# A GLA and MLP-mixer kernel on one core: a second hand order of all instructions and loads

## The chip, the cores and the metric

The kernel runs on one core of a Trainium2 chip. The metric is device time in microseconds (us); lower is better. Every execution is one launch of the whole program.

## The reference

Two stages follow each other, for 4 batches, 8 heads, 768 steps and head size 48:

```python
# gated linear attention, per batch and head
for t in range(768):
    state = alpha[t][:, None] * state + outer(k[t], v[t])      # 48 x 48
    y[t] = q[t] @ state
x = y.transpose(0, 2, 1, 3).reshape(4, 768, 384)
# mixer
h  = maximum(x.transpose(0, 2, 1) @ w_tok1, 0) @ w_tok2        # tokens 768 -> 256 -> 768
u  = x + h.transpose(0, 2, 1)
h2 = maximum(u @ w_ch1, 0) @ w_ch2                             # channels 384 -> 1536 -> 384
out = u + h2
```

Inputs, weights and the output are float32.

## The kernel before

The attention is cut into 12 blocks `n` of 256 steps: three for each batch, so blocks 0 to 2 belong to batch 0 and blocks 9 to 11 to batch 3. A block has two halves (0 and 1) of 128 steps. Each operation has a name that ends in its block. In order of their dependence:

- `ld_at`, `ld_kt`, `ld_qt`, `ld_vt`: loads of alpha, k, q and v (384 KB each, issued by SP). `ldw_` loads a weight, `cw_` casts it to bf16 (L745 on ACT, L746 on DVE and POOL).
- `P`, `ln1`, `lnP`, `r1` (`ln` in blocks 0 to 2): products and logarithms of alpha. `cum` (`cumw`): cumulative sums by matmul. `E`, `IE`: their exponentials, on ACT.
- `k0a`, `q0r`: one factor into k and q (L692, L696). `kk`, `qq`: the scaled k and q (L700). `vb`, `vs`, `ka`, `kb`, `kc`: casts and copies between partitions.
- Blocks 0 to 5: `trk`, `trq`: transposes by PE (L712), and `evk`, `evq` bring them out of PSUM. Blocks 6 to 11: `dk`, `dq`: transposes by DMA (L725), and `pq` rearranges q's.
- `G0_`, `G1_`: the products of k and q of a half; `mask0_`, `mask1_` (DVE, L770) mask them. `K`: the sum of k times v; `s0_`, `sa`, `sm`: the new state. `i`, `y`: the output by matmul, `x` brings it out of PSUM.

The mixer of batch `b` has token matmuls `t1` and `t2` (L878, L883) with `ht` and `u` (L887) behind them; transposes of u (`up` and `ut` for batch 0, `ux` by DMA, L729, for the others); channel matmuls `c1_b_mc_half` (L902) into one PSUM bank each, `rt` behind them (L873 on ACT, L875 on DVE), `c2_b_i_q` (L907) in quarters, `o` (L911) and the store `st` (L624). The last tile of batch 3 is cut into two halves, `h0` and `h1`. In `c1` the halves of w_ch1 (`wc10` to `wc12` and `wc13` to `wc15`) serve the channel groups 0 to 5 and 6 to 11.

Nothing is scheduled when the program runs. A string `ORDER` lists every operation in the order in which it is emitted; the last letter is its queue: t PE, s ACT, v DVE, g POOL, y SP. Each queue runs its instructions in this order, and waits where an input or a buffer isn't there yet. `f3_trk0` is a filler: matmuls on zeros, as long as three of 512 columns, into a bank that nobody reads. A second list, `BUFS`, gives the buffer number of each value when it first appears (19 buffers for loads, 20 for `rt`, 8 banks of PSUM). So a load on SP waits until the last reader of its buffer is done, and all loads, transposes and stores behind it on SP wait with it. `GATES` is empty.

Copies and products on DVE and POOL that share a port take turns: each one waits for the last of the other engine that stands ahead of it in `ORDER`. This is made in `shared`:

```python
e, last = self.port_turn, self.port_last
if e:
    if last and last[0] != e:
        self.tc.add_manual_dep(i.ins, last[1].ins.name, ..., reason="shared port")
    self.port_last = (e, i)
```

It holds for P, k0a, q0r, kk, qq, vb, vs, ka, kb, kc, pq, sm and the weight casts, where they are on DVE or POOL.

Of the kernel before, what the change touches and what calls it, by code (L numbers as in the profile page):

```python
# [965 lines left out]
```

## Time and profile before

| what | value |
|---|---|
| time, median of 3 runs | 166.03 us (163.29 to 166.45) |
| time of the profiled execution | 164.76 us |
| its span, first to last instruction | 163.0 us |
| PE busy | 155.2 us, 95% of the span |
| DVE busy | 118.0 us, 72% |
| ACT busy | 95.7 us, 59% |
| POOL busy | 74.3 us, 46% |
| share of the chain that ended last: L907, L902 | 14% and 8%, both PE |
| read from HBM, written | 25.17 MB, 4.72 MB |

The span is counted from the first to the last instruction; the time of the execution is a little longer. Rows of a profile give a line of the kernel, an engine, an operation, and the tiles as out<-in. Matmuls are pipelined: the record of one of 384 columns is about 0.33 us long, while the next one starts sooner, so the busy time of PE is that of overlapping records. A value in square brackets is the time that the engine stood idle ahead of a row, with what ended it. Where an instruction waits for several things, the one named came last by the profile.

### The profile page before, as it was taken

The page shows a single profiled execution, that of the slowest core. Times are in us where ns is not written, and L with a number is a line of the kernel's source. Part 1 is how long each engine was busy: PE and PEld are TensorE (multiplying, and loading weights), DVE is VectorE, ACT ScalarE, POOL GpSimd, SP SyncE. Part 2 cuts the span into 40 slices and gives each one's busy share as a digit, 9 for nine tenths or more (in the row PEclk, how much of TensorE's full clock was granted, in tenths as well). Part 3 has the DMA queues.
Part 4 walks back from the last instruction along what each step waited for, and adds up shares of the span by engine and source line. Part 5 has one row for each costly group of instructions (what it writes and reads, how often), then busy time and mean ns, then how long its engine had stood idle before and what let it go on. Part 6 is the DMA issues. An engine that isn't in the chain of part 4 may idle for free. (4 is left out here: it accounts for less than half of the span.)

```text
span 163.0 us, 3969 instructions
## 1 busy us (share of the span) xinstructions
PE 155.2 (95%) x1560; PEld 97.2 (60%) x1560; DVE 118.0 (72%) x214; ACT 95.7 (59%) x178; POOL 74.3 (46%) x87
## 2 busy tenths in 40 slices
PE   7999989799999999999999999999799999999992
PEld 2456555556677676666666656666566655666661
DVE  6299993989989877587969855895698657162622
ACT  3888999789999964487777441495813201721000
POOL 5015593729294867469454278886830100000000
DMA  5999899989999999999999899989730136101133
GB/s 128 325 325 322 225 365 380 314 286 313 300 342 368 264 286 246 238 238 264 149 253 302 217 333 215 227 213 170 160 129 20 36 78 171 57 0 52 53 117 121
DMA packets 76130, 35.05 MB, mean 215 GB/s; under 512 B 70352, under 2 KB 74320, under 8 KB 76112
## 3 DMA queue, kind: packets, MB, share of 16 engines
q1 hardware_dynamic: 74960, 33.33, 77.9%
q10 hardware_dynamic: 1152, 1.48, 2.6%
q8 instruction: 12, 0.20, 0.5%
q14 instruction: 6, 0.05, 0.1%
HBM read 25.17 MB, written 4.72 MB: 183 GB/s over the span
## 5 line engine op out<-in xcount | busy, mean ns | idle before, releaser
L907 PE MATMUL ps<-wc,rt 128*128 128x384 bf16 (+1 forms) x300 | 52.4, 320 | 0.2 <-ACT rt L873 0.2
L902 PE MATMUL ps<-ut,wc 128*128 128x384 bf16 x288 | 50.3, 326 | 0.3 <-POOL wc L746 0.3
L907 PEld LDWEIGHTS <-rt 128*128 128x128 bf16 x300 | 28.0, 98 | 16.5 <-ACT rt L873 0.3
L902 PEld LDWEIGHTS <-wc 128*128 128x128 bf16 x288 | 27.1, 98 | 17.5 <-POOL wc L746 0.5
L873 ACT ACTIVATE rt<-ps 128x384 bf16<-128x384 f32 x54 | 24.9, 491 | 20.2 <-PE ps L902 19.6
L875 DVE TENSOR_SCALAR rt<-ps 128x384 bf16<-128x384 f32 x42 | 21.9, 553 | 12.7 <-PE ps L902 12.7
L770 DVE TENSOR_TENSOR gtm<-ps,mk 128x1024 bf16<-128x1024 f32 x24 | 28.4, 1217 | 1.7 <-PE ps L643 1.6
L911 DVE TENSOR_TENSOR o<-ps,u 128x384 f32<-128x384 f32 (+1 forms) x25 | 13.1, 535 | 5.9 <-PE ps L907 5.8
L887 DVE TENSOR_TENSOR u<-ps,x 128x384 bf16<-128x384 f32 x24 | 11.9, 550 | 6.4 <-PE ps L883 5.6
L700 POOL TENSOR_TENSOR pkk<-in,IE 128x768 bf16<-128x768 f32 x7 | 12.7, 1815 | 2.8 <-DVE in L692 2.5
L745 ACT CAST vb<-in 64x384 bf16<-64x384 f32 (+1 forms) x18 | 11.8, 654 | 2.5 <-DMA in<-in_v_dram 2.2
L643 PE MATMUL ps<-rt 128*64 128x384 f32 (+1 forms) x26 | 11.4, 537 | 1.1 <-DVE rt L541 1.1
L844 POOL TENSOR_TENSOR ss<-tmp,E 128x384 bf16<-128x384 f32 x9 | 7.5, 833 | 9.3 <-DVE tmp L841 9.1
L745 ACT CAST x<-ps 128x384 bf16<-128x384 f32 x15 | 7.0, 477 | 7.5 <-PE ps L643 7.5
L746 POOL CAST vb<-in 64x384 bf16<-64x384 f32 (+1 forms) x14 | 8.3, 594 | 5.8 <-PE ps L643 2.4
L878 PE MATMUL ps<-x,wt 128*128 128x384 bf16 x48 | 10.6, 325 | 0.3 <-ACT wt L745 0.3
L700 POOL TENSOR_TENSOR pkq<-in,E 128x768 bf16<-128x768 f32 x5 | 9.1, 1815 | 2.9 <-ACT IE L679 1.9
L692 POOL TENSOR_TENSOR in<-in,in 128x384 f32<-128x384 f32 x7 | 6.9, 998 | 6.3 <-DVE kt L746 3.2
L643 PE MATMUL ps<-tpq,tpk 48*64 48x128 bf16 (+1 forms) x288 | 8.5, 219 | 1.3 <-POOL tpq L746 0.8
L841 DVE TENSOR_TENSOR tmp<-ps,ss 128x384 f32<-128x384 f32 x16 | 8.8, 552 | 1.0 <-PE ps L643 0.4
L628 POOL TENSOR_TENSOR in<-in 128x384 f32<-128x384 f32 x8 | 7.9, 997 | 3.4 <-DVE ss L844 1.7
L883 PE MATMUL ps<-ht,wt 128*128 128x384 bf16 x48 | 9.3, 326 | 0.1
(95 smaller groups left out, 211.9 us busy)
## 6 DMA issues: line engine op xcount, KB each, us to landing
in<-in_alpha_dram SPq DMA_DIRECT2D x12, 384.0 KB, 5.8
in<-in_k_dram SPq DMA_DIRECT2D x12, 384.0 KB, 5.7
in<-in_q_dram SPq DMA_DIRECT2D x12, 384.0 KB, 5.1
in<-in_v_dram SPq DMA_DIRECT2D x12, 384.0 KB, 5.9
...
```

The lines of the kernel that those rows point to most:

```text
L643: return self.pe.matmul(out, lhsT=lhsT, rhs=rhs, start=start, stop=stop, skip_group_check=True)
L700: self.shared(self.eng[e].tensor_tensor(self.t(dst)[:, :, h0:h1, 0:D], self.t(src)[:, h0:h1].rearrange("p h s d -> p s h d"), bass.AP(tens ...
L745: return self.act.copy(d, s)
L770: self.nc.vector.tensor_tensor(self.t(gtm)[:, hf, :, :], self.pair(gp).rearrange("p a (j t) -> p (a j) t", t=128), bass.AP(tensor=m.tensor ...
L873: self.act.activation(d, s, AF.Relu)
L875: self.nc.vector.tensor_scalar_max(d, s, 0.0)
L878: self.pe.matmul(self.bank(bank)[:, 0:HD], lhsT=self.wt1[:, kc, m * 128 : m * 128 + 128], rhs=self.t(x), start=(kc == 0), stop=(kc == NS - 1))
L883: self.pe.matmul(self.bank(bank)[:, 0:HD], lhsT=self.wt2[:, kc, i * 128 : i * 128 + 128], rhs=self.t(hts[kc]), start=(kc == 0), stop=(kc = ...
L887: self.nc.vector.tensor_tensor(self.t(u)[:, i % 3], self.bank(bank)[:, 0:HD], self.t(x), ALU.add)
L902: self.pe.matmul(self.bank(bank)[:, 0:HD], lhsT=self.wc1[:, kc, mc * 128 : mc * 128 + 128], rhs=self.t(ut)[:, 3 * half : 3 * half + 3, kc, ...
L907: self.pe.matmul(self.bank(bank)[:, 0 : cz - ca], lhsT=self.t(rts[mc][0])[:, i * 128 : i * 128 + 128], rhs=self.wc2[:, mc, ca:cz], start=( ...
L911: self.nc.vector.tensor_tensor(self.t(o)[:, ca:cz], self.bank(bank)[:, 0 : cz - ca], self.t(u)[:, i % 3, ca:cz], ALU.add)
```

## The change

Only `ORDER` and `BUFS` are different; the operations, their sizes and their dependences are the same, apart from the fillers. The order of every queue is another from the first microsecond to the last, many operations change their engine, and buffers are numbered anew. On ACT there are now 196 operations (185 before), on DVE 189 (191), on POOL 69 (75), on SP 96 (99); eleven stores go out on ACT's queue instead of eight. Named by the change itself is the load of block 11's values: `ld_vt11` now stands on SP behind `dq10`. Three stretches of it: the start, the weights and first mixer, and blocks 9 to 11.

```diff
 ORDER = """
-ld_at0y ln0s ld_at1y f8_cumw0t f1_cumw0t cumw0t ln1s ld_kt0y IE0s cumw1t kk0v kb0v ld_qt0y E0s qq0v ld_vt0y IE1s vb0s
-ka0g f3_trk0t trk0t evk0v vs0_0v f3_trq0t trq0t kc0v vs1_0v E1s ld_kt1y kk1v f4_K0t K0t s0_0v sa1_0v evq0s f2_G0_0t
-G0_0t G1_0t ib0t mask1_0v ld_at2y ka1s ln2s ld_vt1y vb1s kb1g trk1t cumw2t IE2s kc1s sm1_0g ld_qt1y qq1v f3_trq1t
-trq1t vs0_1g E2s mask0_0v vs1_1s y1_0t f4_K1t K1t evq1v sa0_1v y0_0t ld_kt2y kk2g trk2t evk1s ld_qt2y qq2v G1_1t
-f1_trq2t trq2t x1_0s evk2s sm0_1v sa1_1v ld_vt2y G0_1t vb2g mask1_1v kc2g mask0_1v sm1_1g evq2s vs0_2s f4_K2t f1_K2t
-K2t x0_0s G0_2t G1_2t ld_at3y P3g ldw_wt11y cw_wt11s ib1t y1_1t vs1_2g sa0_2v mask0_2v ldw_wt10y cw_wt10s ia1t y0_1t
-t1_0_0_0t t1_0_0_1t x1_1s ia2t x0_1s y0_2t sm0_2g ib2t t1_0_1_0t t1_0_1_1t ld_at4y ln14s t1_0_1_2t x0_2s mask1_2v
-t1_0_1_3t y1_2t ldw_wt21y t1_0_0_2t x1_2v t1_0_0_3t t1_0_0_4t t1_0_1_4t t1_0_1_5t cw_wt21s P4g lnP4s ldw_wt20y
-cw_wt20g ht_0_1v t1_0_0_5t ld_kt3y k0a3v lnP3s cum3t ldw_wc15y ht_0_0s ldw_wc13y ldw_wc14y t2_0_2t t2_0_3t ld_vt3y
-t2_0_5t t2_0_1t u_0_2v t2_0_0t IE3s cum4t ln13s r13s u_0_3v up_0_1t E3s kk3g cw_wc15g t2_0_4t u_0_5v trk3t IE4s u_0_1v
-u_0_0v up_0_0t u_0_4v up_0_2t ut_0_0v ut_0_1s ut_0_2v cw_wc13g cw_wc14s c1_0_11_0t rt_0_11_0v vb3g vs0_3v E4s
-c1_0_8_1t ld_qt3y ka3s q0r3v ldw_wc11y kb3v evk3s ldw_wc10y c1_0_9_1t kc3s c1_0_10_1t qq3v rt_0_10_1v c1_0_8_0t
-ldw_wc12y cw_wc11g rt_0_8_1s vs1_3s rt_0_9_1s c1_0_11_1t cw_wc10g rt_0_8_0v rt_0_11_1v c1_0_10_0t rt_0_10_0s trq3t K3t
-ld_at5y ld_kt4y c1_0_9_0t evq3s c1_0_7_0t cw_wc12g ld_qt4y ld_vt4y s0_3v r14s ld_kt5y sa1_3v sm1_3g G0_3t rt_0_9_0s
-G1_3t mask0_3v mask1_3v rt_0_7_0s c1_0_1_1t c1_0_5_0t c1_0_0_1t ln15s c1_0_2_0t P5g c1_0_5_1t rt_0_5_0s rt_0_2_0v r15s
-rt_0_1_1s rt_0_5_1v rt_0_0_1s lnP5s c1_0_7_1t rt_0_7_1s c1_0_6_1t rt_0_6_1s c1_0_4_0t c1_0_3_1t k0a4g kk4v cum5t ib3t
-y1_3t c1_0_1_0t q0r4v qq4v c1_0_3_0t vb4s IE5s ka4v k0a5g E5s rt_0_3_1v trq4t rt_0_3_0v x1_3s trk4t evk4v rt_0_1_0s
-c1_0_2_1t rt_0_2_1v evq4s ldw_wc20y kb4s cw_wc20g c1_0_4_1t rt_0_4_0v G0_4t ld_qt5y q0r5g mask0_4v ldw_wc21y ld_vt5y
...
-u_2_5v u_2_4v ld_qt10y ux_2_1y lnP10s o_1_3v lnP11s c2_1_5_0t st_1_3y c2_1_5_1t c2_1_0_0t u_2_0v ln111s cum11t
-c2_1_0_1t c2_1_0_2t dq9y t2_2_1t u_2_1v cum10t c2_1_0_3t E11s k0a10g IE10s u_2_2v q0r10g E10s c2_1_5_2t c2_1_5_3t
-o_1_4v IE11s o_1_5v c1_2_10_1t kb9g rt_2_10_1v c1_2_7_1t rt_2_7_1v kk10g o_1_0v pq9v c1_2_1_1t c1_2_3_1t c1_2_8_1t
-vs0_9s qq10g ux_2_0y rt_2_8_1s c1_2_11_1t c1_2_0_0t dk9y c1_2_11_0t rt_2_3_1s G1_9t rt_2_11_1v G0_9t ka9s rt_2_1_1v
-ld_qt11y rt_2_0_0s r111s rt_2_11_0v vs1_9s mask1_9v c1_2_10_0t c1_2_9_0t c1_2_3_0t c1_2_6_0t rt_2_10_0s mask0_9v
-rt_2_6_0v kk11g kc9s K9t s0_9v rt_2_3_0s rt_2_9_0s c1_2_5_0t c1_2_1_0t c1_2_7_0t st_1_4y q0r11g c1_2_9_1t ib9t
-rt_2_5_0s rt_2_7_0v ld_vt11y vb11s rt_2_1_0v y1_9t rt_2_9_1s dq10y c1_2_8_0t rt_2_8_0s c1_2_5_1t rt_2_5_1s sa1_9v
-c1_2_4_0t rt_2_4_0s c1_2_2_0t qq11g c1_2_2_1t rt_2_2_1v pq10g dk10y G1_10t vb10s G0_10t mask1_10v sm1_9g mask0_10v
-y0_9t c1_2_0_1t vs0_10g dk11y rt_2_2_0s c2_2_0_0t c2_2_0_1t c2_2_0_2t c2_2_0_3t x1_9v rt_2_0_1v o_2_0v dq11y kb10s
-pq11g vs0_11v st_2_0y vs1_10s x0_9s G0_11t G1_11t mask0_11v c2_2_2_0t c2_2_1_0t c2_2_2_1t c2_2_2_2t ka10g ia10t y0_10t
-kc10s mask1_11v st_1_0s x0_10s K10t vs1_11g c2_2_2_3t sa0_10v sm0_10v sa1_10v c2_2_1_1t t1_3_0_0t t1_3_0_1t c1_2_6_1t
-kc11s c2_2_1_2t c2_2_1_3t sm1_10v st_1_5y K11t sa0_11v ib10t y1_10t rt_2_6_1s t1_3_0_2t t1_3_1_0t t1_3_1_1t ia11t
...
+ld_at0y ln0s ld_at1y ln1s ld_kt0y f8_cumw0t f1_cumw0t cumw0t IE0s E0s kk0v cumw1t IE1s ld_qt0y ld_vt0y f3_trk0t trk0t
+qq0v f1_trq0t trq0t ka0s kc0v E1s vb0v vs0_0s kb0v vs1_0v f3_K0t K0t ld_kt1y kk1v ka1g s0_0v evk0v evq0s f6_G1_0t
+G1_0t ld_at2y ld_vt1y trk1t ln2s cumw2t sa1_0v vb1s kb1g sm1_0g evk1s IE2s mask1_0v ib0t y1_0t kc1v ld_qt1y qq1v G0_0t
+x1_0v f1_trq1t trq1t vs0_1s mask0_0v vs1_1s E2s ld_kt2y kk2g K1t f1_y0_0t y0_0t sa0_1v sm0_1v evq1s trk2t kc2s sa1_1v
+f3_G1_1t G1_1t G0_1t ib1t ld_qt2y qq2g sm1_1g x0_0s ldw_wt10y cw_wt10s mask1_1v f2_trq2t trq2t ld_vt2y vb2s vs0_2g
+f3_K2t K2t evq2s ldw_wt11y y1_1t x1_1s ldw_wt20y evk2v cw_wt11g cw_wt20g mask0_1v sa0_2v sm0_2g G0_2t G1_2t ia1t y0_1t
+vs1_2s ia2t t1_0_0_0t t1_0_1_0t t1_0_1_1t mask0_2v t1_0_0_1t y0_2t x0_1s t1_0_0_2t t1_0_1_2t t1_0_1_3t ib2t ld_at3y
+t1_0_0_3t P3g ln13s x0_2s mask1_2v y1_2t ldw_wt21y cw_wt21g x1_2s t1_0_0_4t t1_0_1_4t f1_t1_0_1_5t t1_0_1_5t t1_0_0_5t
+ht_0_1v lnP3s ht_0_0s cum3t IE3s t2_0_2t u_0_2v r13s ld_at4y ln14s P4g lnP4s t2_0_1t u_0_1v ld_kt3y k0a3g ldw_wc13y
+t2_0_0t t2_0_3t t2_0_4t u_0_0v cum4t u_0_4v u_0_3v E3s t2_0_5t u_0_5v kk3g up_0_0t ut_0_0v cw_wc13s up_0_1t ut_0_1v
+up_0_2t trk3t ldw_wc15y IE4s ldw_wc14y cw_wc15g ut_0_2v cw_wc14s c1_0_10_0t ldw_wc11y ka3s c1_0_11_0t evk3v kc3v
+ld_vt3y cw_wc11s rt_0_10_0v ld_qt3y c1_0_8_1t vb3s E4s r14s rt_0_8_1v kb3g vs1_3g c1_0_7_1t rt_0_7_1v vs0_3v
+c1_0_11_1t rt_0_11_1s c1_0_6_1t rt_0_11_0s q0r3v qq3v rt_0_6_1v ldw_wc12y c1_0_9_0t rt_0_9_0s c1_0_8_0t cw_wc12g
+rt_0_8_0s c1_0_9_1t ldw_wc10y rt_0_9_1v ld_at5y P5g K3t cw_wc10s trq3t s0_3v c1_0_10_1t sa1_3v sm1_3g evq3s ld_kt4y
+c1_0_1_1t rt_0_1_1v c1_0_2_0t rt_0_10_1s rt_0_2_0s G1_3t G0_3t ln15s c1_0_2_1t mask1_3v lnP5s rt_0_2_1s c1_0_3_1t
+k0a4g rt_0_3_1s mask0_3v c1_0_4_1t ld_vt4y rt_0_4_1v vb4s c1_0_1_0t ld_qt4y kk4v rt_0_1_0s c1_0_6_0t r15s c1_0_0_1t
+rt_0_0_1s c1_0_7_0t ldw_wc20y rt_0_7_0s c1_0_5_1t cum5t ib3t E5s q0r4v rt_0_6_0s vs0_4v qq4v trk4t c1_0_4_0t IE5s
...
+c2_1_0_1t ht_2_1v t2_2_5t t2_2_3t u_2_3v t2_2_4t c2_1_0_2t ld_qt9y q0r9g u_2_5v c2_1_4_3t ld_kt11y u_2_4v t2_2_2t
+u_2_2v r111s ux_2_1y t2_2_0t u_2_0v t2_2_1t lnP11s c2_1_5_0t c2_1_5_1t c2_1_5_2t c2_1_5_3t st_1_3y c2_1_0_3t u_2_1v
+vs1_9s qq9v c1_2_1_1t c1_2_3_1t rt_2_3_1s o_1_4v c1_2_10_1t rt_2_1_1v vs0_9s ux_2_0y c1_2_11_1t c1_2_8_1t o_1_1v qq10g
+rt_2_8_1s vb10v dk9y kc9s c1_2_10_0t c1_2_1_0t rt_2_10_1v dq9y c1_2_11_0t st_1_4y c1_2_0_0t rt_2_11_1s c1_2_9_0t
+rt_2_10_0s k0a11v o_1_5v rt_2_11_0s cum11t vs0_10v rt_2_1_0s c1_2_7_1t IE11s rt_2_9_0v pq9g G1_9t o_1_0v G0_9t E11s
+c1_2_3_0t rt_2_0_0s c1_2_9_1t rt_2_3_0s c1_2_2_0t rt_2_9_1s mask1_9v mask0_9v c1_2_0_1t K9t s0_9v c1_2_5_0t sa1_9v
+rt_2_2_0s st_1_1y kk10g rt_2_0_1s c1_2_4_0t c1_2_8_0t c1_2_2_1t vs1_10g rt_2_4_0s rt_2_5_0s rt_2_2_1v c1_2_6_0t
+rt_2_6_0v c1_2_7_0t ld_qt11y rt_2_8_0s ib9t y1_9t y0_9t c2_2_0_0t rt_2_7_1s q0r11g qq11g kk11g dq10y pq10s ka10s x1_9v
+c2_2_0_1t dk10y sm1_9v rt_2_7_0s kb10g G1_10t G0_10t mask0_10v dq11y x0_9s st_1_0s pq11g c1_2_4_1t rt_2_4_1s c2_2_0_2t
+t1_3_1_0t ia10t t1_3_1_1t y0_10t x0_10s dk11y c1_2_6_1t c2_2_0_3t ld_vt11y vb11s mask1_10v G0_11t vs0_11s G1_11t
+st_1_5y rt_2_6_1v o_2_0v mask0_11v c2_2_2_0t kc10g K10t c2_2_2_1t sa0_10v sm0_10v sa1_10v mask1_11v sm1_10g c1_2_5_1t
+rt_2_5_1s c2_2_2_2t c2_2_2_3t kc11v c2_2_1_0t vs1_11s o_2_2v ib10t y1_10t c2_2_1_1t c2_2_1_2t K11t sa0_11v ia11t
...
 """
 BUFS = """
-12 1 9 0 0 0 0 0 2 6 2 1 0 0 17 0 0 1 2 0 2 2 5 12 1 2 2 2 0 0 4 5 0 4 0 3 0 1 1 0 7 2 1 0 3 15 1 0 0 1 1 1 1 3 0 0 5
...
+8 0 4 1 0 0 0 1 0 0 2 0 1 18 1 4 4 1 5 5 0 0 6 6 2 1 0 0 0 0 0 0 3 8 2 0 4 2 0 0 1 1 1 0 3 7 1 6 0 0 2 5 2 0 3 3 1 2 1
...
 """
```

More of the change, by code (lines that the diff above doesn't have):

```diff
@@ new lines @@
+ln110s r110s r19s c2_1_2_2t c2_1_3_2t c2_1_3_3t G1_7t G0_7t mask1_7v c2_1_1_0t P10g mask0_7v ld_at11y ib7t ld_qt10y
+q0r10g c2_1_2_3t o_1_2v y1_7t x1_7s c2_1_4_0t c2_1_1_1t G1_8t G0_8t o_1_3v st_1_2s lnP10s ld_kt9y mask0_8v ia7t y0_7t
+c2_1_1_2t kc8s c2_1_4_1t ia8t y0_8t K8t mask1_8v x0_7s c2_1_4_2t cum10t E10s t1_2_0_0t t1_2_0_1t t1_2_1_0t t1_2_1_1t
+t1_2_0_2t sa0_8v t1_2_1_2t sm0_8v ib8t ld_vt9y P11v k0a9g x0_8s y1_8t t1_2_0_3t ln111s IE10s ld_kt10y t1_2_1_3t
+t1_2_1_4t c2_1_1_3t t1_2_0_4t k0a10g kk9g x1_8s t1_2_1_5t ld_vt10y vb9s t1_2_0_5t ka9g ht_2_0s kb9s c2_1_0_0t
@@ new lines @@
+c2_2_5_0t c2_2_3_2t c2_2_5_1t c2_2_5_2t c2_2_3_3t u_3_0v c2_2_5_3t o_2_4v c1_3_3_1t rt_3_3_1s o_2_5v c1_3_8_1t
+rt_3_8_1v st_2_5s c1_3_1_1t rt_3_1_1v ux_3_0y c1_3_0_0t c1_3_4_0t rt_3_0_0v c1_3_9_1t rt_3_4_0v c1_3_6_0t rt_3_6_0s
+o_2_3v c1_3_5_1t c1_3_8_0t rt_3_5_1s rt_3_8_0s st_2_0y c1_3_11_0t c1_3_2_0t st_2_4y rt_3_2_0s c1_3_2_1t c1_3_4_1t
+rt_3_11_0s rt_3_9_1s c1_3_7_1t c1_3_10_1t c1_3_10_0t c1_3_0_1t c1_3_7_0t rt_3_2_1v rt_3_7_1v c1_3_11_1t st_2_3s
+rt_3_7_0v rt_3_0_1s c2_3_4_0t c1_3_5_0t c1_3_1_0t c1_3_6_1t rt_3_5_0s c2_3_3_0t rt_3_6_1v rt_3_11_1v rt_3_4_1s
```

61 lines of the change are left out of this document (26 added, 35 removed), and 20 rows, old and new, of the table BUFS.

## The prediction

> **What bounds the kernel now.** I read the page's first part, then the busy time by stretch of the span, then the chain that ended last, then the timeline of each engine up to the first channel matmul.
>
> ```profile
> span 163.0 us, 3969 instructions
> PE 155.2 (95%) x1560; PEld 97.2 (60%) x1560; DVE 118.0 (72%) x214; ACT 95.7 (59%) x178; POOL 74.3 (46%) x87
> ```
>
> ```profile
> 0.00:32.92 32.92, 29.59 (x315) 16.76 (x315) 25.20 (x57) 26.92 (x41) 15.99 (x29) 1.00 1.01 298
> 32.92:48.80 15.88, 15.79 (x158) 10.27 (x159) 14.79 (x25) 14.79 (x28) 9.64 (x12) 1.00 1.05 309
> 103.00:117.10 14.10, 13.15 (x160) 8.27 (x159) 10.39 (x17) 9.85 (x21) 11.30 (x9) 1.00 1.01 199
> 32.92:159.95 127.03, 125.62 (x1246) 80.47 (x1246) 92.41 (x158) 68.74 (x138) 58.33 (x59) 1.00 0.77 196
> 159.95:163.04 3.09, 0.00 (x0) 0.00 (x0) 0.36 (x1) 0.00 (x0) 0.00 (x0) 1.00 0.27 96
> ```
>
> ```profile
> 136.48 10.24 PE ps L902 x63
> ```
>
> Columns of the second fence: length, then busy time of PE, PEld, DVE, ACT and POOL, granted clock, DMA share, GB/s. 95% busy alone would not prove that PE sets the end. The chain does: 63 matmuls of 384 columns in 10.24 us are 0.163 us each, back to back. So the span has three parts. From 32.92 (the first c1, L902) to 159.95 PE idles 127.03 - 125.62 = 1.4 us in all. Behind it stand 3.09 us of last addition and store. Before it stand 32.92 us, in which PE is not the bound:
>
> ```profile
> 1.05 4.04 PE L643 MATMUL ps<-rt 128*64 128x384 f32 x7 [1.05 <-DVE rt L541]
> 19.90 1.40 PE L643 MATMUL ps<-rt 128*64 128x384 f32 x4
> 29.74 0.81 PE L894 MATMUL ps<-idn,u 128*128 128x128 bf16 x6 [0.32 <-DVE u L887]
> 31.22 0.62 PE L712 MATMUL ps<-idn,pkk 128*128 128x128 bf16 x8 [0.35 <-POOL pkk L700]
> 32.92 3.57 PE L902 MATMUL ps<-ut,wc 128*128 128x384 bf16 x21 [0.35 <-POOL wc L746]
> ```
>
> The rt rows are fillers, whose output nobody reads; the last three rows wait for DVE and POOL. Hence a new order can gain in two places only: an earlier first c1, and those 1.4 us.
>
> **The change part by part.** *What stays.* The PE instructions ahead of the first c1 are the same set in both orders (fillers aside), so those behind it are too. Behind the first c1 only stalls can differ. The tail ends as before (two half tiles of o_3_0, a store): 3.1 us in both. Eleven stores instead of eight are issued on ACT:
>
> ```profile
> 160.34 0.34 ACTq L624 DMA_DIRECT2D out_dram<-o  x1
> ```
>
> Three times 0.34 is 1 us on an engine that behind 32.92 is busy for 68.74 of 127.03; I cost it at nothing, and at 1 us if it fell into the first mixer, where no store stands. Fillers go from 34 units of 512 columns to 33. They lie in waits of PE and I cost them at nothing; without that cover one unit is about 0.2 us.
>
> *The first 25 us.* The loads come in nearly the same order, and DVE has the same masks and sums. What differs cancels:
>
> ```profile
> 12.98 1.21 DVE L770 TENSOR_TENSOR gtm<-ps,mk 128x1024 bf16<-128x1024 f32 x1
> 14.11 0.95 DVE L700 TENSOR_TENSOR pkq<-in,E 128x768 bf16<-128x768 f32 x1
> 18.72 0.55 DVE L844 TENSOR_TENSOR ss<-tmp,E 128x384 bf16<-128x384 f32 x1
> 22.58 2.35 DVE L770 TENSOR_TENSOR gtm<-ps,mk 128x1024 bf16<-128x1024 f32 x2
> 19.52 1.31 ACT L745 COPY tpq<-ps 128x1024 bf16<-128x1024 bf16 x1
> 15.76 1.82 POOL L700 TENSOR_TENSOR pkk<-in,IE 128x768 bf16<-128x768 f32 x1
> ```
>
> evk0 moves behind K0 and s0_0 on DVE, but the copies vb0 and kc0 now stand where it stood; adding the durations I reach the first mask at 12.95 against 12.98. After it come kc1 and x1_0 (0.8 us more on DVE than before), while evq1 (1.3) leaves for ACT and the state sums of block 1 come before mask1_1: the state is ready at 18.4 instead of 19.9. That gain is lost again: evq2 on ACT now stands behind cw_wt10 and vb2 and ends at 22.1 instead of 20.8, and block 2's first mask needs it. So the last mask of block 2 ends at 24.9 in both.
>
> *25 us to the first c1.* Here lies the gain.
>
> ```profile
> 26.66 0.56 DVE L875 TENSOR_SCALAR ht<-ps 128x384 bf16<-128x384 f32 x1 [0.41 <-PE ps L878]
> 28.66 0.56 DVE L692 TENSOR_TENSOR in<-in,in 128x384 f32<-128x384 f32 x1 [1.44 <-DMA in<-in_moe_w_ch_dram]
> 29.13 2.87 DVE L887 TENSOR_TENSOR u<-ps,x 128x384 bf16<-128x384 f32 x6
> 32.22 1.02 DVE L746 COPY ut<-ps 128x768 bf16<-128x768 bf16 x2 [0.21 <-PE ps L894]
> 26.83 0.49 ACT L873 ACTIVATE ht<-ps 128x384 bf16<-128x384 f32 x1
> 31.28 0.90 ACT L745 CAST wc<-in 128x768 bf16<-128x768 f32 x1
> 24.03 1.00 POOL L628 TENSOR_TENSOR in<-in 128x384 f32<-128x384 f32 x1
> 29.35 1.81 POOL L700 TENSOR_TENSOR pkk<-in,IE 128x768 bf16<-128x768 f32 x1 [2.55 <-DVE in L692]
> 31.11 1.72 POOL L746 CAST wc<-in 128x768 bf16<-128x768 f32 x2
> ```
>
> The second row is k0a3: DVE stands 1.44 us for a load (the row names a weight load that was in flight as well; k0a3 reads k and alpha), with six finished or nearly finished u additions queued behind it, and the ut copies and the first c1 behind those. The change puts k0a3 on POOL. DVE is then free for u_0_2 as soon as t2_0_2 is done. My sum: mask ends 24.9, y1_2 0.35, x1_2 on ACT 0.5, the last t1 and ht 0.5 each: t2 starts at 26.85. u_0_2 starts at 27.3, six u take 2.87; the last, u_0_5, stands behind cum4, which waits for P4 and four short ACT steps, and ends at 30.15. Two ut copies take 1.02: 31.2, against 32.92 before.
>
> The other inputs of this c1 are three wc casts. POOL now has P3, cw_wt21, P4, k0a3, kk3, cw_wc15 in a row: from 23.9, with 1.0, 0.82, 1.0, 1.0, 1.82 and 0.86, to 30.4, if its loads are there. What is late next is the load of k3 and wc14. In both orders wc14 is the 22nd load. The load queue's rows:
>
> ```profile
> 9.04 1.11 SPq L584 DMA_DIRECT2D in<-in_q_dram  x1
> 11.01 0.51 SPq L584 DMA_DIRECT2D in<-in_k_dram  x1
> 20.67 0.52 SPq L584 DMA_DIRECT2D in<-in_k_dram  x1
> 21.23 2.81 SPq L605 DMA_DIRECT2D in<-in_moe_w_ch_dram  x3
> 26.83 6.19 SPq L605 DMA_DIRECT2D in<-in_moe_w_ch_dram  x3
> ```
>
> Before, a load went out every 1.15 us or so, and once 2 us passed (9.04 to 11.01: its buffer was held by vs1_0). In the new order that hold meets nobody, but ldw_wt21 waits for cw_wt10, which I put at 20.05 on ACT, and every load stands behind it. At the pitch of the undisturbed issues wc14 lands about 29.3 and c1 starts at 31.2. If the loads come as late as before, k3 only just ahead of its 28.66 row, then k0a3, kk3 and cw_wc15 end at 31.9 and c1 starts at 32.0. The bounds are 31.2 and 32.0; I take 31.4, near the first, because the hold is gone. Gain 1.5 us.
>
> *The first mixer.* ACT and DVE are both 93% busy (14.79 of 15.88), and the evictions free PE's banks. Adding up, with durations like those above (less 0.09 us, by which records in a row overlap), what is queued on each until the first c2 is possible: DVE 14.0 us (12.6 in the old order; evq4 and x1_3 come to it), ACT 14.1 (14.7), for 15.4 us of PE. I went through the bank that each c1 takes over: it is free in time each time, the closest being K3 (rt_0_9_0 ends 0.2 us ahead), G1_3 and G0_4 (evq3 and evq4 end with nothing to spare). No stall.
>
> *Blocks 9 to 11.* Before, POOL had 11.30 us of work in 14.10 and G1_10 stood:
>
> ```profile
> 106.31 1.81 POOL L700 TENSOR_TENSOR pkq<-in,E 128x768 bf16<-128x768 f32 x1 [0.91 <-issue]
> 114.42 1.33 POOL L746 COPY tpq<-tpk 128x1024 bf16<-128x1024 bf16 x1 [1.51 <-DMA tpk<-pkq]
> 115.80 0.64 PE L643 MATMUL ps<-tpq,tpk 48*64 48x128 bf16 x32 [0.85 <-POOL tpq L746]
> DMA to landing us min/median/max: 2.7/3.1/6.1
> ```
>
> That is most of the 1.4. The change gives pq10 to ACT and qq9 and k0a11 to DVE, and puts pq9 on POOL ahead of kk10. It also sends vt11's load behind dq10 and three more transposes; by my sum it lands at about 117, and K11, which needs it through vb11 and two copies, stands at 121.4. If that cover is gone, each us of it costs one. Due times here are 31.2 plus the PE work that lies between the first c1 and the instruction. pq9 is the tight one: t2_2_1 is done at 97.4, so u_2_1 at 98.0 and qq9 at 98.9; dq9 goes out behind ux_2_0 and dk9 at 100.7, lands with 2.7 to 3.1 at 103.4 to 103.8, pq9 ends near 105.2, and G1_9 is due at 105.3. Behind it kk10, vs1_10, q0r11, qq11, kk11, kb10, pq11 and kc10 (9.5 us) wait on POOL; they end at 115, K10 is due at 117.2. I allow 0.3 us of idle in place of 1.4: gain 1.1, with ends of 1.4 (none) and minus 3 (dq9 at 6.1).
>
> *Sum.* 163.0 - 1.5 - 1.1 = 160.4 span. The profiled execution took 164.76, 1.8 above its span: 162.2. That execution lies 0.8% under the median shown, 166.03 (163.29 to 166.45), so 162.2 is 1.6% under its own time and 2.3% under the median.
>
> *A rule weighed.* The granted clock reads 1.00 in every stretch above, yet the first seven filler records take 4.04 us and four like them at 19.90 take 1.40: by its pace PE begins at well under full rate and has it later. The Trainium skill, "TensorE: Matmul & The Clock Gate", part 1, says that an idle window of some 3.4 us halves the clock until the PE has been busy again. The pace of the first fillers agrees; the granted clock does not show it. The new order has thinner fillers ahead of trq0, K0, K1 and K2, and this rule speaks against that. By my walk no gap of PE there exceeds 1 us, so the sum by the rule is the same; the case where it is not stands below.
>
> **The rivals.**
>
> *The loads set the first c1 as before, and the rest evens out.* For it: DMA share 1.01 up to 32.92. Against: the 2.55 and 1.44 us of idle on POOL and DVE, which have their place in the order. c1 at 32.0 to 32.9, stalls as before: 163.8 to 164.8, centre 164.4.
>
> *pq9 blocks POOL.* For it: the transposes' 6.1 us. Against: in the new order the loads are issued earlier and fewer stand ahead of dq9. 3.4 us on G1_9: 165.6.
>
> *Slower: the evictions become the bound in the first mixer (33 to 48 us).* Its ACT queue holds three instructions that wait for a load (cw_wc11, vb3, cw_wc10) with rt evictions behind each, and DVE has vs0_3 and kk4, which wait for POOL. ACT has 1.3 us to spare, DVE 1.4. If each of the five stands as long as k0a3 did (1.44), 7.2 us go, 5.8 of them on PE: 168.0. If each stands as long as kk3 did on POOL (2.55), 12.8 go, 11.4 on PE: 173.6. Centre 170.8. It decides from 1.3 us of waiting, and makes the kernel slower than the median from 5.2. For it: 93% on both engines. Against: the same share before cost PE 0.09 us in that stretch.
>
> *The clock falls back.* One window of 3.4 us at half rate costs at most 1.7 us: 163.9. For it only the thinner fillers; against it the gaps under 1 us.
>
> **How the numbers follow.** 2% is about what a measurement of this kernel can tell from no change: under 162.7 is faster, over 169.4 slower. The forecast has 0.58, with a range of its own from 160.2 (no stall, c1 at 31.0) to 164.0; 0.45 of it lies under 162.7, 0.13 above. The loads as before 0.09, pq9 0.05 and the clock 0.02 are all within 2%. The evictions have 0.26, of which 0.22 lie over 169.4: five waits are only those I can name, and the later mixers have the same pattern. Sums: faster 0.45, same 0.13 + 0.16 + 0.04 = 0.33, slower 0.22. The range, 160.0 to 169.5, leaves out about 0.2, nearly all of it above.
>
> **What would show it.** Right: k0a3 on POOL, u additions starting near 27.4, the first c1 between 31.2 and 32.0, G1_10 without idle, PE idle behind the first c1 under 1 us, the same 3.1 us of tail. Wrong: a first c1 after 32.9; bank waits on L902 between 32 and 47 (PE idle released by rt evictions); G1_9 after 106 with POOL idle ahead of pq9's end; cw_wt10 after 21, which moves every load.

## The result and the profile after

Over 20 runs of each, taken together, the kernel before has a median of 164.44 us and the changed kernel 163.49; the ratio is 0.9944 (95% interval 0.9921 to 0.9966). So the change gains 0.95 us, 0.6%. In a later pair on one chip the ratio was 0.9978 (0.9948 to 1.0008), a gain that isn't clear of noise. The forecast was 162.2, a gain of 2.6 us on the profiled execution's own time: the sign is right and the size is not. The page of the changed kernel:

```profile
span 161.2 us, 3965 instructions
PE 155.0 (96%) x1559; PEld 96.9 (60%) x1559; DVE 116.9 (73%) x212; ACT 100.0 (62%) x186; POOL 70.1 (43%) x81
```

The same three stretches as in the prediction (length, then busy time of PE, PEld, DVE, ACT and POOL, granted clock, DMA share, GB/s):

```profile
0.00:32.29 32.29, 29.48 (x314) 16.59 (x315) 24.21 (x57) 26.66 (x41) 17.55 (x28) 1.00 1.03 301
32.29:158.12 125.83, 125.47 (x1246) 80.29 (x1245) 92.37 (x155) 73.38 (x146) 52.52 (x53) 1.00 0.74 199
158.12:161.20 3.08, 0.00 (x0) 0.00 (x0) 0.36 (x1) 0.00 (x0) 0.00 (x0) 1.00 0.27 96
```

First c1 starts at 32.29 instead of 32.92, PE idles 0.36 us behind it instead of 1.4, and the tail is the same 3.1. These two profiles are 1.8 us apart, twice the distance of the medians. Each shows one execution, and the experiments had to tell how much of the difference belongs to the order.

The timelines of the changed kernel ahead of first c1 (DVE, POOL, ACT, then PE):

```profile
28.43 2.88 DVE L887 TENSOR_TENSOR u<-ps,x 128x384 bf16<-128x384 f32 x6 [1.14 <-PE ps L883]
31.22 1.47 DVE L746 COPY ut<-ps 128x768 bf16<-128x768 bf16 x3
26.87 1.00 POOL L692 TENSOR_TENSOR in<-in,in 128x384 f32<-128x384 f32 x1
30.84 0.89 ACT L745 CAST wc<-in 128x768 bf16<-128x768 f32 x1 [0.28 <-DMA in<-in_moe_w_ch_dram]
27.43 1.78 PE L883 MATMUL ps<-ht,wt 128*128 128x384 bf16 x10 [0.21 <-ACT ht L873]
29.44 0.49 PE L883 MATMUL ps<-ht,wt 128*128 128x384 bf16 x2
32.29 0.97 PE L902 MATMUL ps<-ut,wc 128*128 128x384 bf16 x5
```

k0a3 is on POOL as planned, but the six u additions start at 28.43, not near 27.4, and wc14's cast waits for its load until 30.84. A t2 is a pair of matmuls and takes 0.49 us (29.44), so t2_0_2 ends at 27.92; u_0_2 starts half a microsecond later still. Around G1_10 (SP, ACT, PE):

```profile
106.17 2.33 SPq L725 DMA_TRANSPOSE tpk<-pkq  x1
113.26 1.38 ACT L745 COPY tpq<-tpk 128x1024 bf16<-128x1024 bf16 x1
115.16 0.64 PE L643 MATMUL ps<-tpq,tpk 48*64 48x128 bf16 x32
```

G1_10 has no idle time in front of it.

### The profile page after: what moved, and what is told of

Same layout as the page of the kernel before. It is cut to its first block, busy times and chain, and to the rows that moved or that the text cites. A ratio compares the mean times of both kernels' runs of the same rounds, so it can differ in the third digit from the quotient of the medians.

```text
span 161.2 us, 3965 instructions
## 1 busy us (share of the span) xinstructions
PE 155.0 (96%) x1559; PEld 96.9 (60%) x1559; DVE 116.9 (73%) x212; ACT 100.0 (62%) x186; POOL 70.1 (43%) x81
## 4 chain that ended last, share of the span: by engine, by line
PE 71%; DMA 8%; DVE 7%; ACT 7%; SPq 3%; issue 1%
PE ps L907 29%; PE ps L902 24%; PE ps L643 9%; DMA in<-in_moe_w_ch_dram 4%; PE ps L878 4%; PE ps L883 4%; DMA in<-in_alpha_dram 3%; DMA out_dram<-o 2%; SPq L605 1%; ACT IE L687 1%; SPq L584 1%; PE ps L712 1%; DVE pkk L700 1%; DVE vb L746 1%; DVE o L911 1%
## 5 line engine op out<-in xcount | busy, mean ns | idle before, releaser
L907 PE MATMUL ps<-wc,rt 128*128 128x384 bf16 (+1 forms) x300 | 53.5, 319 | 0.0
L873 ACT ACTIVATE rt<-ps 128x384 bf16<-128x384 f32 x60 | 27.3, 495 | 26.6 <-PE ps L902 26.4
L770 DVE TENSOR_TENSOR gtm<-ps,mk 128x1024 bf16<-128x1024 f32 x24 | 28.5, 1218 | 1.5 <-PE ps L643 1.2
L875 DVE TENSOR_SCALAR rt<-ps 128x384 bf16<-128x384 f32 x36 | 18.9, 552 | 11.8 <-PE ps L902 11.8
L700 POOL TENSOR_TENSOR pkk<-in,IE 128x768 bf16<-128x768 f32 x6 | 10.9, 1819 | 3.5 <-DVE ss L844 1.7
L700 POOL TENSOR_TENSOR pkq<-in,E 128x768 bf16<-128x768 f32 x6 | 10.9, 1817 | 2.5 <-ACT vb L745 1.4
L745 ACT CAST x<-ps 128x384 bf16<-128x384 f32 x17 | 8.1, 477 | 5.5 <-PE ps L643 5.4
L746 POOL COPY kt<-pkk 64x384 bf16<-64x384 bf16 x7 | 3.5, 503 | 12.9 <-DVE pkk L700 9.1
L692 POOL TENSOR_TENSOR in<-in,in 128x384 f32<-128x384 f32 x8 | 8.0, 999 | 2.1 <-DVE in L628 1.6
L643 PE MATMUL ps<-vb,gtm 128*128 128x48 bf16 x192 | 8.6, 183 | 0.2 <-DVE gtm L770 0.2
L643 PEld LDWEIGHTS <-tpk 48*64 48x64 bf16 (+1 forms) x288 | 5.9, 102 | 4.8 <-issue 1.9
```

What stands on the lines that cost most here:

```text
L643: return self.pe.matmul(out, lhsT=lhsT, rhs=rhs, start=start, stop=stop, skip_group_check=True)
L700: self.shared(self.eng[e].tensor_tensor(self.t(dst)[:, :, h0:h1, 0:D], self.t(src)[:, h0:h1].rearrange("p h s d -> p s h d"), bass.AP(tens ...
L745: return self.act.copy(d, s)
L770: self.nc.vector.tensor_tensor(self.t(gtm)[:, hf, :, :], self.pair(gp).rearrange("p a (j t) -> p (a j) t", t=128), bass.AP(tensor=m.tensor ...
L873: self.act.activation(d, s, AF.Relu)
L875: self.nc.vector.tensor_scalar_max(d, s, 0.0)
```

## The experiments

**The named part alone (b_vt11), and undone (a_vt11).**

```diff
 # before, SP's queue (vb11 moves back with its load)
-ld_vt11y ... dq10y
+dq10y ld_vt11y
```

> The kernel before with the named part of the change alone: block 10's transposed queries (dq10) are put ahead of the load of block 11's values (vt11) on SP. Theory N, that vt11's load ahead of dq10 is what makes it land late: dq10 lands at about 113.3 instead of 114.29, G1_10's stall of about 1.0 us before its start at 115.80 goes, and the time falls by 0.8 to 1.0 us (0.5 to 0.6%). Rival, that dq10 waits for qq10, which POOL ended only at 108.12, and that its latency of about 6.1 us is its own: dq10 still lands 6.1 us after 108.1, G1_10 stalls as before, and the time changes by less than 0.2 us.

Its timelines (SP, PE):

```profile
108.05 1.23 SPq L725 DMA_TRANSPOSE tpk<-pkq  x1
109.38 0.54 SPq L584 DMA_DIRECT2D in<-in_v_dram  x1
115.08 0.64 PE L643 MATMUL ps<-tpq,tpk 48*64 48x128 bf16 x32
```

dq10 is issued 0.1 us earlier than before and lands at 112.55 instead of 114.29. G1_10 does not stall: between c1_2_2_0 and c2_2_1_2, two PE instructions on either side of it, pass 9.43 us, against 10.34, 10.03 and 10.14 in three profiles of the kernel before. Time: 0.9969 of before (0.9935 to 1.0003), about 0.5 us. The trace shows the mechanism of theory N with its size. The time agrees with it, but its interval just reaches 1. This execution wasn't a short one either (span 162.3): first c1 started at 31.88, and PE then stood for a weight cast, whose load came late:

```profile
49.48 0.32 PE L907 MATMUL ps<-wc,rt 128*128 128x384 bf16 x1 [0.88 <-ACT wc L745]
```

```diff
 # changed kernel, SP's queue
-dq10y ... dk11y ... ld_vt11y
+ld_vt11y dq10y ... dk11y
```

> The changed kernel with the named part undone: vt11's load is issued ahead of dq10 on SP again. Theory N: dq10 lands about 1 us later, the G1_10 matmul, which started at 115.15 with no stall, stalls by 0.5 to 1.0 us, and the time rises by 0.4 to 0.9 us. Rival, that dq10's landing 6.2 us after its issue is its own and that the gain came from qq10 ending at 102.8 instead of 108.1: G1_10 starts within 0.2 us of 115.15 and the time does not move.

SP, ACT and PE:

```profile
109.60 0.39 SPq L584 DMA_DIRECT2D in<-in_v_dram  x1
110.09 1.59 SPq L725 DMA_TRANSPOSE tpk<-pkq  x1
114.35 1.35 ACT L745 COPY tpq<-tpk 128x1024 bf16<-128x1024 bf16 x1 [0.78 <-DMA tpk<-pkq]
115.75 0.64 PE L643 MATMUL ps<-tpq,tpk 48*64 48x128 bf16 x32 [0.35 <-ACT tpq L745]
```

A stall is back, though a smaller one (0.35 us, against 0.54 to 0.85 in the kernel before); pq10 on ACT does not prevent it. It came in another way than theory N said. The load was issued only at 109.60, and dq10 stood behind it on SP until 110.09, 3.9 us later than in the changed kernel; it then landed 4.2 us after its issue, sooner than the changed kernel's 6.2. Time: 0.9981 (0.9954 to 1.0008) against 0.9944, 0.6 us slower. But the intervals overlap, and in its later pair the changed kernel stood at 0.9978, so the times alone don't show what the undone move costs.

**The early part alone on the kernel before (b_early).**

```diff
-k0a3v ... ut_0_1s ... cw_wc13g cw_wc14s
+k0a3g ... cw_wc13s ... ut_0_1v ... cw_wc14s
```

> The kernel before with the early part of the change done by itself: k0a3 on POOL instead of VectorE, cw_wc13 on ScalarE ahead of cw_wc14 instead of POOL, ut_0_1 on VectorE instead of ScalarE. Theory of two paths (the u additions and the copies of the last loaded weight blocks meet at first c1): the u additions start at about 28.4 instead of 29.1, the first c1 matmul starts at 32.3 to 32.4 instead of 32.92, the time falls by 0.4 to 0.6 us. Rival, that the loads alone set first c1: it stays within 0.15 us of 32.92 and the time does not move.

```profile
28.51 2.88 DVE L887 TENSOR_TENSOR u<-ps,x 128x384 bf16<-128x384 f32 x6 [1.13 <-PE ps L883]
32.60 1.62 PE L902 MATMUL ps<-ut,wc 128*128 128x384 bf16 x9 [0.65 <-DVE ut L746]
```

u came at 28.5 as expected and first c1 at 32.60, 0.2 later than expected. The time did not fall: 1.0043 of before (1.0008 to 1.0077). The theory of two paths does not explain a loss. The profiles below give a likely reason: 32.92 was not what the kernel before always does. In this execution kt3's load landed at 26.51; with landings at 26.26 and 26.78, the untouched early order has first c1 at 31.45 and 31.88. This is argued from single executions, and this one (163.40 us) was the fastest of the version's 12, whose median is 164.83.

**k0a3 back on VectorE in the changed kernel (a_k0a3v).**

```diff
-... t2_0_2t u_0_2v ... u_0_1v ld_kt3y k0a3g
+... t2_0_2t ... ld_kt3y k0a3v u_0_2v u_0_1v
```

> The changed kernel with k0a3 back on VectorE, ahead of the six u additions. If kt3's load lands by 27 us (four of the six profiles so far): k0a3 doesn't stall, and as VectorE is then busy when the first u's wait is over, u_0_2 starts 0.1 to 0.2 us behind t2_0_2's end instead of 0.5 us; first c1 as in the changed kernel or up to 0.3 us earlier. If it lands at 28.2 or later (two of six): u_0_2 at 29.1 or later, first c1 at 32.9 to 33.2. Over the runs the time is within 0.3% of the changed kernel's. By the forecast's step, that k0a3 on VectorE holds the u additions back by 1.5 us in each execution, it is 0.6 to 0.9% slower than the changed kernel, whatever kt3 does.

```profile
27.79 0.56 DVE L692 TENSOR_TENSOR in<-in,in 128x384 f32<-128x384 f32 x1 [0.67 <-DMA in<-in_k_dram]
28.27 2.87 DVE L887 TENSOR_TENSOR u<-ps,x 128x384 bf16<-128x384 f32 x6
```

kt3 landed at 27.31 here, between the two cases. 0.9951 (0.9921 to 0.9980), against the changed kernel's 0.9944: the move of k0a3, the main reason for 1.5 us in the forecast, is worth nothing that can be measured (the intervals are about 0.5 us to either side).

**More profiles of both kernels (b_look2, b_look3, a_look2, a_look3, a_again).** No edit.

> The kernel before, looked at a second time. If the landing of kt3's load varies between executions, first c1 is at 31.8 to 32.0 with kt3 landed by 27 us and no stall of k0a3, and at 32.8 to 33.0 with kt3 landed at 28 us or later; if the stall of 1.44 us is the order's own, it is there again and first c1 is at 32.9 either way. G1_10 stalls by 0.9 to 1.1 us in both cases.

> The kernel before, a third look. First c1 at 31.9 with kt3's load landed by 27 us, at 32.6 to 32.9 with it landed at 27.8 or later; G1_10 stalls by 0.4 to 1.0 us. The mean of first c1 over the profiles with this early order then stays within 0.4 us of the mean with the new one (32.3).

> The changed kernel, looked at a second time. First c1 at 32.1 to 32.7 (the three runs with its early order have 32.29, 32.67 and 32.12), the first u 0.5 us behind t2_0_2's end, PE idle behind first c1 under 1 us. If the changed kernel's gain at first c1 were the 0.63 us of the first pair of profiles, it would be at 32.3 or before; if it is about 0.15 us on average, anywhere in that range.

> The changed kernel, a third look. First c1 at 32.1 to 32.7. qt11's load lands at 109.8 to 111.3; where it lands after 110.2, pq11 ends at 117.7 or later and G0_11 stalls by 0.2 to 0.6 us; where it lands before 110, as in the first profile, pq11 ends by 117.3 and G0_11 does not stall.

VectorE of the second and then of the third profile of the kernel before:

```profile
28.43 0.56 DVE L692 TENSOR_TENSOR in<-in,in 128x384 f32<-128x384 f32 x1 [1.53 <-DMA in<-in_moe_w_ch_dram]
26.94 0.56 DVE L692 TENSOR_TENSOR in<-in,in 128x384 f32<-128x384 f32 x1
27.72 2.88 DVE L887 TENSOR_TENSOR u<-ps,x 128x384 bf16<-128x384 f32 x6 [0.22 <-PE ps L883]
```

One program, two executions: with kt3 landed at 27.95, k0a3 stands 1.53 us and first c1 starts at 32.69; with kt3 at 26.26, k0a3 does not stand at all and first c1 starts at 31.45. All profiles whose order up to first c1 is exactly that of one of the two kernels (x_ba and x_ab follow below):

| order up to first c1 | chip | kt3 landed | first c1 |
|---|---|---|---|
| before (profile of the prediction) | not recorded | 28.17 | 32.92 |
| before, b_look2 | 4 | 27.95 | 32.69 |
| before, x_ba | 4 | 27.80 | 32.55 |
| before, b_vt11 | 12 | 26.78 | 31.88 |
| before, b_look3 | 12 | 26.26 | 31.45 |
| changed | not recorded | 26.75 | 32.29 |
| changed, a_look2 | 13 | 27.35 | 32.22 |
| changed, a_look3 | 12 | 26.47 | 32.32 |
| changed, a_again | 12 | 27.14 | 32.20 |
| changed, a_vt11 | 12 | 26.54 | 32.67 |
| changed, x_ab | 4 | 27.29 | 32.12 |

Both means are 32.30, but from five and six executions, of which those of before differ by 1.5 us. The old order follows kt3's load; the new one does not, and pays for that in the executions in which the load is early. What decides between early and late is open: with the old order the early landings were all on chip 12 and, where the chip is recorded, the late ones on chip 4, so it may be the chip as well as the execution, and the equal means hang on this mix. For the execution speak the times on chip 12 alone: next to each other there, before ranged from 162.71 to 164.77 us (22 runs) and the changed kernel from 162.81 to 163.87 (12 runs).

The load behind the other input of first c1, wc14, came no sooner in the new order. It landed at 31.07, 30.95 and 30.03 in three profiles of before, and at 30.81, 31.43, 30.06 and 30.55 in four of the changed kernel; both means are 30.7.

Behind first c1 (second and third profile of before; then the second and third of the changed kernel and a_again):

```profile
32.69:158.91 126.22, 125.38 (x1246) 80.39 (x1246) 92.18 (x157) 68.71 (x138) 58.31 (x59) 1.00 0.75 198
31.45:158.33 126.88, 125.82 (x1246) 80.30 (x1246) 92.42 (x157) 69.25 (x139) 58.50 (x59) 1.00 0.77 197
32.22:158.49 126.27, 125.82 (x1246) 80.25 (x1245) 92.46 (x155) 73.63 (x148) 52.57 (x53) 1.00 0.75 199
32.32:158.23 125.91, 125.51 (x1246) 80.30 (x1245) 92.37 (x155) 72.91 (x146) 52.56 (x53) 1.00 0.74 197
32.20:158.27 126.07, 125.50 (x1246) 80.04 (x1245) 92.53 (x155) 73.13 (x146) 52.58 (x53) 1.00 0.75 200
```

With the first profiles, PE idles 1.4, 0.8 and 1.1 us there in three executions of before and 0.4, 0.5, 0.4 and 0.6 in four of the changed kernel. The mean falls from 1.10 to 0.45 us. Idle time ahead of G1_10 makes the difference: 0.85 in the first profile of before, and in its second and third

```profile
114.79 0.64 PE L643 MATMUL ps<-tpq,tpk 48*64 48x128 bf16 x32 [0.54 <-POOL tpq L746]
114.22 0.64 PE L643 MATMUL ps<-tpq,tpk 48*64 48x128 bf16 x32 [0.65 <-POOL tpq L746]
```

**The seam (x_ba, x_ab).** Up to 54 us one kernel's order, the other's behind it:

```diff
-ORDER = before
+ORDER = before[:318] + (the changed kernel's order of all other operations)   # x_ba; x_ab the other way, at 333
```

> The first 318 operations in the order and on the engines of the kernel before (to about 54 us: loads of blocks 0 to 4, first gather, first mixer's c1), all others in the order and on the engines of the changed kernel. Theory L, that the change gains behind 54 us alone and its early part gives nothing or costs a little (k0a3 stalls VectorE only in executions in which kt3's load lands late; in the one with vt11's load moved, kt3 landed at 26.78 and first c1 was at 31.88 with the early order of before): at least as fast as the changed kernel, 0.988 to 0.996 of before. Rival E, the forecast's, that first c1 earlier by the new early order is half of the gain: 0.996 to 0.999.

> The opposite: the first 333 operations of the changed kernel (to about 54 us), all others as in the kernel before. Theory L: no gain or a small loss, 0.998 to 1.004 of before, and G1_10 stalls as in before by about 1 us. Rival E: 0.994 to 0.997.

Both theories missed: 1.0231 (1.0190 to 1.0271) and 1.0283 (1.0224 to 1.0342). A stall behind the seam in x_ba, and one in x_ab:

```profile
57.00 0.40 PE L643 MATMUL ps<-tpq,tpk 48*128 48x128 bf16 x8 [1.32 <-DVE gtm L770]
73.48 1.79 PE L902 MATMUL ps<-ut,wc 128*128 128x384 bf16 x10 [1.88 <-DMA ut<-u]
```

The two orders don't fit together: each half expects what the other half of its own order has done already. So the times of these two tell nothing of the halves' worth, and their first 33 us are used only for the table above.

**The first u addition waits for one engine instead of two (a_swapu).**

```diff
-t2_0_2t u_0_2v ... t2_0_1t u_0_1v
+t2_0_1t t2_0_2t u_0_1v u_0_2v
```

> The changed kernel with u_0_1 ahead of u_0_2 (and their matmuls), so that the first of the six u additions adds an x1 of VectorE's own and waits for TensorE alone, not for TensorE and ScalarE. Theory that the 0.47 us between the end of the wait and u_0_2's start at 28.43 is the price of that second wait and that the u additions bind at first c1: the six begin at about 28.0, first c1 starts at about 31.8 instead of 32.29, the time falls by 0.3 to 0.5 us. Rival, that the last load (wc14, landed at 30.8, its copy done at 31.7) binds just as late: first c1 moves by less than 0.2 us.

PE, then VectorE:

```profile
28.16 1.79 PE L883 MATMUL ps<-ht,wt 128*128 128x384 bf16 x10 [0.21 <-ACT ht L873]
28.68 2.88 DVE L887 TENSOR_TENSOR u<-ps,x 128x384 bf16<-128x384 f32 x6 [0.67 <-PE ps L883]
```

u starts 0.03 us behind the end of its t2 (28.16 + 0.49), not 0.51, so the half microsecond is gone. But all ran later in this execution, wc14 landed at 31.37, and first c1 was at 32.54: it came no earlier, as the rival had it. 0.9935 (0.9905 to 0.9965), no different from the changed kernel's 0.9944.

**Where the stall goes (a_both, a_qt11, a_qt11_2).** In the second profile of the changed kernel qt11's load landed at 110.70 (109.85 in the first) and a new stall stands ahead of G0_11 (POOL: q0r11, pq11; PE: G0_11):

```profile
110.86 1.00 POOL L696 TENSOR_TENSOR in<-in,lf 128x384 f32<-128x384 f32 x1 [1.08 <-ACT rt L873]
117.49 1.33 POOL L746 COPY tpq<-tpk 128x1024 bf16<-128x1024 bf16 x1 [0.72 <-DMA tpk<-pkq]
118.87 0.64 PE L643 MATMUL ps<-tpq,tpk 48*64 48x128 bf16 x32 [0.20 <-DVE rt L875]
```

q0r11 starts 0.16 us behind the landing; its row names an ACT eviction, whose result it does not use. G0_11 starts 0.05 us behind pq11's end (118.82); the eviction that its row names ended in the same moment, but frees another bank. In the third profile the load landed at 109.42 and G0_11 did not stall. The recorded idle time is not all that this costs: between c1_2_2_0 and c2_2_1_2 pass 14.49 us in the second profile, 13.91 and 13.92 in the first and third.

```diff
 # a_swapu, SP's queue: a_both, then a_qt11
-st_1_4y ... st_1_1y ... ld_qt11y ... dq10y
+ld_qt11y dq10y st_1_4y ... st_1_1y
+st_1_4y ld_qt11y dq10y ... st_1_1y
```

> The changed kernel with u_0_1 ahead of u_0_2 (as in the run with the u additions exchanged) and, on SP, qt11's load and block 10's transposed queries (dq10) ahead of the two stores st_1_4 and st_1_1. Theory N, that a transpose lands late when a 393 KB load was issued shortly before it, and that POOL's chain q0r11, qq11, kk11, kb10, pq11 starts when qt11 lands: qt11's load is issued at about 104.6 instead of 105.7, dq10 at 105.1; dq10 lands by 111.5 (6.2 to 7.0 us behind its issue in the changed kernel's runs, since the load is still just ahead of it), G1_10, G0_11 and G1_11 start without a stall, and the time is 0.1 to 0.4% under the run with the u additions exchanged alone: 0.989 to 0.993 of before. Rival, that these stalls are as small on average as in the changed kernel's first profile: 0.993 to 0.996.

VectorE and PE of a_both:

```profile
111.69 0.56 DVE L911 TENSOR_TENSOR o<-ps,u 128x384 f32<-128x384 f32 x1 [4.91 <-DMA out_dram<-o]
112.30 2.08 PE L902 MATMUL ps<-ut,wc 128*128 128x384 bf16 x6 [4.46 <-DVE o L911]
```

1.0316 (1.0259 to 1.0372). I had moved a store past a load and a transpose without asking who waits for it: st_1_4 left at 107.08 and landed at 111.67, o_1_0 needs its buffer, and the masks and evictions of VectorE, then PE, stood behind o_1_0.

> The changed kernel with u_0_1 ahead of u_0_2 and, on SP, qt11's load and dq10 ahead of the store st_1_1 alone (st_1_4, whose buffer o_1_0 needs next, stays ahead of both). Theory that the stall has moved from G1_10 to G0_11, because POOL's chain q0r11, qq11, then dq11 and pq11 starts when qt11 lands: its load is issued 0.5 us earlier, q0r11 starts 0.3 to 0.6 us earlier than the mean of the changed kernel's runs (110.8), G0_11's stall of 0.4 to 0.6 us shrinks to 0.2 or less, no new stall at o_1_0, and the time is 0.990 to 0.994 of before. Rival, that the landing varies more than that: 0.993 to 0.996, as the run with the u additions exchanged.

> The version with u_0_1 ahead of u_0_2 and qt11's load and dq10 ahead of st_1_1, again, next to the changed kernel on the same chip. If G0_11's stall (0.24 to 0.6 us in profiles of the changed kernel in which qt11 lands after 110) is what it removes: 0.1 to 0.4% faster than the changed kernel, 0.990 to 0.993 of before, and q0r11 starts by 110. If its first 0.9910 was chance: within 0.1% of the changed kernel.

> The changed kernel, timed again next to that version: 0.993 to 0.996 of before, as in its first 20 runs (0.9944). First c1 at 32.2 to 32.7, PE idle behind it 0.3 to 0.8 us.

POOL of the first of these (q0r11, pq11), and the stretch behind first c1 of the second:

```profile
109.86 1.01 POOL L696 TENSOR_TENSOR in<-in,lf 128x384 f32<-128x384 f32 x1
115.83 1.34 POOL L746 COPY tpq<-tpk 128x1024 bf16<-128x1024 bf16 x1
32.02:157.63 125.61, 125.44 (x1246) 80.22 (x1245) 92.73 (x155) 73.36 (x147) 52.53 (x53) 1.00 0.74 199
```

With st_1_4 left in front, q0r11 no longer waits and PE idles 0.2 us behind first c1. Times: 0.9910 (0.9876 to 0.9943), and measured again 0.9945 (0.9919 to 0.9971) beside the changed kernel's 0.9978: 162.51 against 163.24 us, 12 runs of each. The difference of their means is 0.77 us, with 0.11 as its standard error. This version beats both kernels. It holds two edits, the exchange of the u additions and the new place of qt11's load and dq10; no pair of runs side by side tells what each is worth. Its profile had 0.2 us less at first c1 and 0.4 us less idle behind it than a_again's. In a_again qt11 landed at 109.67 and G0_11 didn't stall, so that stall is not all of it; what else it saves is open.

**What makes kt3 late (b_pe48).**

```diff
 # before, the first filler, of eight units
+if count == 8:
+    for _ in range(48):
+        self.mm(self.bank(bank)[:, 0:16], z, z[:, 0:16], True, True)
+    count = 1
```

> The kernel before with its first fillers (4 matmuls of 384 to 512 columns) replaced by 48 of 16 columns and one of 512: some 45 more matmuls and as many weight loads at the head of TensorE's program, same work behind. Theory C, that the 16 KB packets of the instruction queue q8 bring TensorE's program and that each holds one of the 16 DMA engines back by about a microsecond, so that all loads in flight land that much later by their last sixteenth: the first two packets come 3 to 5 us earlier (from 14.4 to 16 and 25 to 26.5 to about 11 and 22), the last sixteenth of the load in flight then (vt1 or qt1 near 12 to 14, at4 or wt21 near 23 to 25) falls from 0.3 to over 1.2 us behind its middle one, and no longer first at qt2 (16.1) and kt3 (26.2). Rival, that the lag belongs to the loads or to the time: the packets move and the lag stays at qt2 and kt3 or wc15.

The trace has 16 landing records, or parts, for each load; the core has 16 DMA engines. How far the last part of a load lands behind the eighth, in us, with the packets of the instruction queue q8 (each 16 KB, 0.88 to 1.09 us):

```
                 packets at      at2   vt1   qt1   kt2   qt2  ... wt10  wt11   at4  wt21  wt20   kt3
before           14.61, 26.05   0.19  0.24  0.25  0.23  1.46      0.57  0.57  0.51  0.52  0.50  1.58
before, b_look2  14.43, 25.87   0.30  0.29  0.30  0.29  1.35      0.44  0.43  0.40  0.30  0.35  1.70
before, b_vt11   15.88, 26.52   0.33  0.38  0.35  0.46  1.76      0.63  0.63  0.61  0.62  0.64  0.64
b_pe48           11.57, 23.78   0.25  1.56  1.43  1.14  0.76      1.16  1.25  1.11  1.73  1.66  1.61
```

In b_vt11 the load behind kt3, wc15, is the first to lag (1.67). The packets come 3.0 and 2.3 us earlier with more TensorE instructions in front, and the first lag goes with the first packet, from qt2 to vt1. The second is less clean, because loads lagged by 1.1 to 1.25 already ahead of it; it rises to 1.73 at wt21, at the packet's time. So theory C, that TensorE's own program comes in through the DMA engines that carry the loads, holds for the first packet and fits the second. It fits, too, that only one of the sixteen parts is late: of qt2 in the first profile of before, fifteen had landed by 16.34 and the last at 17.59; of vt1 in b_pe48, fifteen by 12.68 and the last at 14.00. The lag is only half of what makes kt3 late, though. Between the first and the third profile of before kt3's landing differs by 1.9 us: 0.9 is the lag of its last part, the other 1.0 its later issue (20.67 against 19.71), which stays open. This execution of b_pe48, the only one, took 166.66 us, with stalls at 73 and 110 us that I have not followed.

## Why the prediction was wrong

*First c1: 1.5 us forecast, 0.63 in the first pair of profiles, none on average.* The step that failed is "DVE stands 1.44 us for a load", read as a property of the order. It belongs to executions in which kt3's load lands at 27.8 or later; with the landing at 26.26 the same program doesn't stand at all (b_look3), and with k0a3 back on VectorE the changed kernel takes no measurably different time (a_k0a3v). The forecast's own new path was too short as well: t2 started at 27.43, not 26.85 (the last mask of block 2 ended at 25.37, not 24.9; the terms given for the rest add up to 26.75), and u_0_2 came 1.00 us behind t2_0_2's start, not 0.45, because t2's own 0.49 us and the half microsecond of the double wait lay in it. "wc14 lands about 29.3" failed by 1.5 us: it landed at 30.06 to 31.43 in four profiles of the changed kernel, though in the first, by the landing records, thirteen of its sixteen parts were there at 29.53. The last part sets the cast. "The hold is gone" leaned too far as well: the wait of wt21 for cw_wt10, which the prediction names, is a longer hold in its place. In the first profile of the changed kernel no load went out between 17.56 and 20.32, and wc14 was issued at 24.81 against 23.60 before. So the rival that the loads set first c1 as before was right about the load: wc14 landed at 30.7 on average in either order.

*Stalls behind first c1: 1.1 us forecast, 1.05 in the first pair, 0.65 on average.* The size holds in the first pair only, and the reason does not hold. I gave the gain to pq10 on ACT and the relief of POOL, and saw in the moved load no gain, only a risk. The run with that move alone takes the stall away (b_vt11), and with the move undone half of it is back while pq10 is on ACT (a_vt11). The risk did not come: vt11's load landed at 120.22, not 117, and PE idled nowhere behind it. And the question "what is late next" had the wrong answer: I named pq9. It is late indeed, behind dq9's landing at 105.98, and G1_9 starts at 107.51, right behind pq9's end (107.46), where 105.3 was given (1.1 of the 2.2 us is first c1's own lateness); but PE had other work, walked wrongly, until then and idles only 0.2 us there. What costs more is pq11 when qt11's load is late: 0.6 us in the second profile.

*The sum.* 163.0 was the longest span of three profiles of before (162.0 and 161.5 are the others): latest first c1, longest idle at G1_10. Subtracting both as if they were always there gave 2.6 us where 0.95 were to be had. Of these the profiles place 0.65 behind first c1; the rest is within their scatter. The median of three runs, 166.03, was 1.6 above that of twenty, so "2.3% under the median" leaned on it too.

*What held.* The tail (3.08), no stall by evictions in the first mixer (PE idles 0.36 us in all the 126 behind first c1), and the granted clock, 1.00 in each stretch with the thinner fillers. The idle window of the rule weighed in the prediction did not come up: from the first filler to first c1, PE's longest gap in the first profile of the changed kernel is 0.26 us. So no run here tests it.
